# An attention and cosine-gated MLP kernel on one core: first k in fp32 by hardware queues, single-bank blocks of h, four output accumulators, a new order of loads

## The chip, the core and the metric

The kernel runs on one core of a Trainium2 chip. The time is device microseconds of one execution. The engines are TensorE (PE; its weight loads are the row PEld), VectorE (DVE), ScalarE (ACT), GpSimd (POOL) and SyncE (SP). Each works through its own list of instructions in order; semaphores order the engines among each other. DMAs are issued from SP and ACT (hardware queues, shown as hardware_dynamic) and from POOL (software queue). Casting fp32 to bf16 while loading is done on POOL's queue alone in this kernel.

## What is computed

Two attention steps, then a two-layer MLP without bias whose gate is a cosine:

```python
def sm_attn(qq, kk, vv):                        # scale = 1/sqrt(64)
    s = scale * np.matmul(qq, kk.transpose(0, 1, 3, 2))
    a = np.exp(s - s.max(-1, keepdims=True))
    return np.matmul(a / a.sum(-1, keepdims=True), vv)
p_packed = sm_attn(p, k, v)                     # p: 8 x 8 x 32 x 64; q, k, v: 8 x 8 x 576 x 64
x = sm_attn(q, p_packed, p_packed)              # then heads side by side: 4608 x 512
h = x @ w_in                                    # 512 x 2048
out = (h * np.cos(h)) @ w_out                   # 2048 x 512
```

Inputs and the output are fp32 in HBM; matmuls are bf16 into fp32 accumulators.

## The kernel before

There are 8 batches of 576 rows. A batch goes through these steps, each a function of the kernel:

- `load` brings k, q or v of a batch as bf16, 96 partitions x 8 heads x 384. `pe_T` (24 transposes on PE into PSUM, three groups of 8, each copied out by an engine that is named) or `xbar` (a transposing DMA issued on SP) makes kT and qT. `permute_v` reorders v.
- `s1`: scores of p against k, exponentials on ACT with their sums. `a1_pe`, `a1_one` or `a1_xbar` transposes them. `pp` multiplies by v and gives ppT (two copies on one engine, two on another). `ppw(b, n)` multiplies ppT by a quarter of w_in, so that PPW holds p_packed times w_in, 2048 columns.
- `s2`: scores of q against p_packed, exponentials. `sums2` and `normalise` divide by the sums, through Ln and Exp on ACT, and give a2n.
- `h_mm(b, fc)`: block fc of 16 of h, transposed: 128 features x 576 rows, as 4 matmuls of 288 columns (2 contraction halves y, 2 halves e of the rows) into a PSUM tile of two banks; ACT takes Sin with a phase of pi/2 (L254), VectorE multiplies it with h into gT (L257). After blocks 7 and 15 POOL copies the last 64 of the 576 rows to `joint`, in which two batches share a chunk of 128 rows.
- `out_gen(b)`: the output product, chunks of 128 rows, 16 matmuls of 512 columns each into one accumulator (L303), then a copy to SBUF and DMAs on SP. It is a generator: `fill(n)` takes n matmuls from it at a chosen place, `set_filler(b)` finishes the last batch's and starts a new one.

The order is written out by hand. First batches 0 and 1 up to their scores; then 16 blocks of h(0), with the rest of ppw(0) behind blocks 1, 5 and 8, pp(1) behind 10, the transposes of q1 behind 11 to 13, and 2 output matmuls behind 14 and 15; then s2(1) to normalise(1) with 22 output matmuls among them; then `slot(1, ...)`: 16 blocks of h(1), behind each its share of output matmuls of batch 0 and what its list of hooks names. The stages of batches 2 to 7 follow the same pattern, h(s) with the output of s − 1.

PSUM has 8 banks: pool A, three tiles of two banks each (`psa`), in turn; pool O, two tiles of one bank (`bank`, the accumulators, some transposes). A tile is taken again when all that read it before have finished.

POOL's list is at first: k0, v0, identity, q0, k1, p, w_in 0 to 2, v1, w_in 3, q1, w_out 0 to 3, p, k2, permute of v1, and later q2, k3, v2. xbar of k2, q2 and k3 stand on SP during h(1); a copy on POOL (`gate`, L444) waits for kT of batch 3, and behind it on POOL stand the load of q3, the permute of v2 and the loads of v3 and k4.

Of the kernel before, what the change touches and what calls it, by code (L numbers as in the profile page):

```python
# [8 lines left out]
FP32 = mybir.dt.float32  # L9
BF16 = mybir.dt.bfloat16  # L10
AF = mybir.ActivationFunctionType
# [4 lines left out]
def kernel(  # L16
# [10 lines left out]
    nc = tc.nc  # L27
# [19 lines left out]
    cos_pool = ctx.enter_context(tc.tile_pool(name="cos", bufs=3))  # L47
    o_pool = ctx.enter_context(tc.tile_pool(name="o", bufs=4))
    small = ctx.enter_context(tc.tile_pool(name="small", bufs=3))
    A = ctx.enter_context(tc.tile_pool(name="psA", bufs=3, space=PSUM))  # L50
    O = ctx.enter_context(tc.tile_pool(name="psO", bufs=2, space=PSUM))

    ctx.enter_context(tc.manual_schedule())
# [21 lines left out]
        else:  # L75
            eng.tensor_copy(out=out, in_=in_)  # L76

    def psa(dt=FP32):
        return A.tile([128, 2, 512 if dt == FP32 else 1024], dt, name="psA", tag="A")
# [161 lines left out]

    def h_mm(b, fc):
        if fc == 0:
            gT[b] = g_pool.tile([128, NFC, S], BF16, name="gT", tag="gT")
            if b % 2 == 0:
                joint[b // 2] = j_pool.tile([128, NFC, 128], BF16, name="joint", tag="joint")
        ps = psa()
        for y in range(2):
            for e in range(2):
                nc.tensor.matmul(ps[:, e, 0:HS], PPW[b][:, y, fc * 128:(fc + 1) * 128],  # L250
                                 a2n[b][:, y, e * HS:(e + 1) * HS], start=(y == 0), stop=(y == 1))
        cs = cos_pool.tile([128, S], BF16, name="cosT")
        csv = cs.rearrange("p (e x) -> p e x", e=2)
        ACT.activation(out=csv, in_=ps[:, :, 0:HS], func=AF.Sin, bias=PI_HALF)  # L254

        def rest():
            V.tensor_tensor(out=gT[b][:, fc, :].rearrange("p (e x) -> p e x", e=2),  # L257
                            in0=ps[:, :, 0:HS], in1=csv, op=ALU.mult)
# [4 lines left out]
        return rest  # L263

    n_out = [0]

# [13 lines left out]
    def n_chunks(b):  # L280
        return 5 if b % 2 and b < B - 1 else 4
# [11 lines left out]
                q.dma_start(out=rows[:, cols], in_=osb[a:z, cols])  # L293

    def out_gen(b):
        groups = [(0, 1), (2,), (3,)] if b == 0 else [(c,) for c in range(n_chunks(b))]
        for grp in groups:
            pss = {c: O.tile([128, DM], FP32, name="ot", tag="ot") for c in grp}
            for f0 in range(0, NFC, 4):
                for c in grp:  # L300
                    for fc in range(f0, f0 + 4):
                        w = joint[b // 2][:, fc, :] if c == 4 else gT[b][:, fc, c * 128:(c + 1) * 128]
                        nc.tensor.matmul(pss[c], w, w_out_bf[:, fc, :],  # L303
                                         start=(fc == 0), stop=(fc == NFC - 1))
                        if fc == NFC - 1:
                            osb = o_pool.tile([128, DM], FP32, name="osb")
                            copy((V, ACT)[n_out[0] % 2], osb, pss[c])
                            n_out[0] += 1
                            for a, z, rows in pieces_of(b, c):
                                nc.sync.dma_start(out=rows, in_=osb[a:z, :])  # L310
                        yield

    filler = [None, 0]
# [44 lines left out]
    for t in a1:  # L358
        V.memset(t[:, :, :, TP:128], 0.0)

    warm(7)
    dup_p(0, 2, V)
    pack_p(0, 1)
    warm(9)
    pe_T("k", 0, (V, ACT, V))
    s1(0)
    permute_v(0, V)
    load("v", 1)
    load_w_in(3)
    warm(3)  # L370
    a1_pe(0)
    warm(2)
# [1 line left out]
    pp(0)  # L374
    pe_T("q", 0, (V, ACT, V))
    load("q", 1)
    for n in range(4):
        load_w_out(n)
    G.dma_start(out=p_raw[:, 4:, :], in_=p_rows[:, 4:, :])
    s2(0)  # L380
    warm(3)
    dup_p(2, 4, V)
    sums2(0, 0)
    sums2(0, 1)
    pe_T("k", 1, (V, V, V))
# [6 lines left out]
    a1_one(1)  # L392
    rest_ppw()
    recips(1)
    load("k", 2)
    permute_v(1)
    for fc in range(NFC):
        h_mm(0, fc)()
        if fc in (1, 5, 8):
            ppw(0, 1 + fc // 4, (ACT, V), own=True)  # L400
        if fc == 10:
            pp(1, own=True, engs=(ACT, ACT))
        if fc in (11, 12, 13):
            pe_T("q", 1, (V, ACT, V), (fc - 11,), own=True)
        if fc == 13:
            set_filler(0)
        if fc >= 14:
            fill(2)

    def slot(s, hooks, keep=0, heavy={}):  # L410
        left = filler[1] - keep
        weight = [1 + heavy.get(fc, 0) for fc in range(NFC)]
        for fc in range(NFC):
            h_mm(s, fc)()
# [18 lines left out]
    ppw(1, 0, V)  # L433
    load("q", 2)
    load("k", 3)
    load("v", 2)
# [7 lines left out]
    G.tensor_copy(out=gate, in_=xT["k", 3][0:1, 0, 0:1])  # L444
    load("q", 3)
    ppw(1, 1, V)
    normalise(1)
    fill(14)
    slot(1, [(3, lambda: pw2(1, 2, (ACT, V))), (6, lambda: pack_p(2, 5)), (8, lambda: pack_p(5, B)),
             (8, lambda: (permute_v(2), load("v", 3), load("k", 4)))], 4)  # L450

    fill(1000)
    set_filler(1)
# [96 lines left out]
```

## Time and profile before

| | us |
|---|---|
| median of 3 runs | 254.21 (254.09 to 254.35) |
| span of the profiled execution | 252.3 |
| PE busy in it | 233.3 (92%), 1981 matmuls |
| ACT busy | 170.5 (68%) |
| DVE busy | 163.0 (65%) |
| POOL busy | 58.4 (23%) |
| DMA engines | 37.67 MB, mean 149 GB/s |
| first matmul of h(0), h(1), s1(2) | 22.73, 45.71, 63.89 |

The profile is one execution on the chip. Times in it count from the span's start. A line such as L254 is a line of the kernel before. A group names engine, operation, what it writes and reads, the shapes, how often, busy time, mean duration, and the idle time of the engine just before with what ended it. Matmul ends are modelled. The span is that of the execution's first to last instruction, and the runs' times lie somewhat above it.

### The profile page before, as it was taken

To read this page: it belongs to the slowest core of one execution; us is meant where nothing else is said; L and a number is where in the kernel's file an instruction comes from. 1 tells how busy PE (TensorE), PEld (TensorE's weight loads), DVE (VectorE), ACT (ScalarE), POOL (GpSimd) and SP (SyncE) were. 2 spreads that over 40 slices of the span, in tenths; PEclk is the share of its full clock that TensorE was granted. 3 is DMA by queue.
4 is the path that set the end of the run, shared out by engine and by line. 5 is a ranking of instruction groups with operands and counts; after the bars stand their busy time and mean duration, and the time that the engine had idled before them with its cause. 6 is when DMAs were issued, how large, how long until landed. Compare 5 with 4: busy or idle time off the path is not lost.

```text
span 252.3 us, 4989 instructions
## 1 busy us (share of the span) xinstructions
PE 233.3 (92%) x1981; PEld 130.7 (52%) x2014; DVE 163.0 (65%) x245; ACT 170.5 (68%) x285; POOL 58.4 (23%) x71
## 2 busy tenths in 40 slices
PE   8786888999969999999999998999899999999993
PEld 3453463566435554465446553565356554665452
DVE  2548996789376977477847675479556874876110
ACT  2366888857558788878886667887877585873000
POOL 8442604200362243104313105020500000000000
PEclk9999999999999999999999999999999999999998
DMA  6999999999999989999999994979471112112133
GB/s 91 202 211 205 205 207 226 200 186 149 191 208 198 176 175 212 220 204 164 225 173 181 180 182 99 175 141 196 97 144 44 42 44 70 36 34 62 50 83 83
DMA packets 65270, 37.67 MB, mean 149 GB/s; under 512 B 37872, under 2 KB 60656, under 8 KB 65248
## 3 DMA queue, kind: packets, MB, share of 16 engines
q0 software_dynamic: 23184, 18.81, 48.8%
q1 hardware_dynamic: 41904, 18.42, 36.8%
q8 instruction: 15, 0.25, 0.4%
q10 hardware_dynamic: 160, 0.13, 0.2%
q14 instruction: 7, 0.06, 0.1%
HBM read 37.22 MB, written 9.44 MB: 185 GB/s over the span
## 4 chain that ended last, share of the span: by engine, by line
PE 74%; DVE 8%; ACT 7%; DMA 5%; issue 2%; POOL 2%; DVEq 0%; POOLq 0%; ACTq 0%
PE ot L303 42%; PE psA L250 22%; DMA w_in_bf<-in_moe_w_in_dram 5%; DVE gT L257 5%; PE psA L201 3%; ACT cosT L254 3%; PE psA L177 2%; PE psA L227 1%; PE ot L289 1%; ACT a2u L219 1%; ACT L489 1%; DVE rs L147 1%; PE psA L128 1%; DVE osb L76 1%; DVE PPW L76 1%
## 5 line engine op out<-in xcount | busy, mean ns | idle before, releaser
L303 PE MATMUL ot<-w_out_bf,gT 128*128 128x512 bf16 x483 | 126.9, 380 | 2.1 <-issue 1.3
L257 DVE TENSOR_TENSOR gT<-psA,cosT 128x576 bf16<-128x576 f32 x128 | 94.1, 754 | 31.1 <-ACT cosT L254 30.0
L254 ACT ACTIVATE cosT<-psA 128x576 bf16<-128x576 f32 x128 | 82.7, 652 | 29.8 <-PE psA L250 28.1
L250 PE MATMUL psA<-a2n,PPW 128*128 128x288 bf16 x512 | 84.0, 286 | 2.5 <-DVE PPW L76 1.0
L303 PEld LDWEIGHTS <-gT 128*128 128x128 bf16 x512 | 48.0, 98 | 42.6 <-issue 6.1
L250 PEld LDWEIGHTS <-PPW 128*128 128x128 bf16 x512 | 49.1, 98 | 36.5 <-issue 3.8
L76 DVE CAST PPW<-psA 128x1024 bf16<-128x1024 f32 (+1 forms) x23 | 25.8, 1128 | 12.1 <-PE psA L201 12.1
L261 POOL COPY joint<-gT 128x512 bf16<-128x512 bf16 x16 | 9.8, 614 | 88.7 <-DVE gT L257 88.7
L76 DVE COPY osb<-ot 128x512 f32<-128x512 f32 (+1 forms) x19 | 12.8, 671 | 16.9 <-PE ot L303 13.8
L74 ACT COPY osb<-ot 128x512 f32<-128x512 f32 (+1 forms) x18 | 10.3, 571 | 18.7 <-PE ot L303 14.1
L76 POOL COPY vp<-vbf 96x3072 bf16<-96x3072 bf16 x7 | 19.2, 2750 | 1.6 <-DMA vbf<-in_v_dram 1.6
L237 DVE SCALAR_TENSOR_TENSOR a2n<-a2u,r,lns 128x576 bf16<-128x576 bf16 x16 | 12.4, 813 | 9.6 <-ACT lns L235 9.6
L229 ACT ACTIVATE lns<-psA 128x576 f32<-128x576 f32 x16 | 10.3, 651 | 5.7 <-PE psA L227 5.3
L137 ACT ACTIVATE a<-psA 128x576 bf16<-128x576 f32 x16 | 10.2, 648 | 5.0 <-PE psA L128 5.0
L303 PE MATMUL ot<-w_out_bf,joint 128*128 128x512 bf16 x46 | 12.4, 380 | 0.1
L201 PE MATMUL psA<-w_in_bf,ppT 64*32 64x512 bf16 x224 | 10.4, 381 | 1.5 <-DVE gT L257 1.1
L219 ACT ACTIVATE a2u<-psA,rs 128x576 bf16<-128x576 f32 x16 | 11.0, 736 | 1.2 <-PE psA L128 1.1
L254 ACT ACT_TABLE_LOAD x8 | 10.3, 1283 | 0.1
L74 ACT CAST ppT<-psA 64x128 bf16<-64x128 f32 x24 | 6.2, 259 | 6.1 <-PE psA L103 2.9
L235 ACT ACTIVATE lns<-lns 128x576 f32<-128x576 f32 x16 | 10.0, 678 | 0.0
L341 PE MATMUL ot<-wz 128*128 128x512 bf16 x24 | 8.1, 472 | 1.5 <-DVE wz L353 1.2
L74 ACT CAST PPW<-psA 128x1024 bf16<-128x1024 f32 (+1 forms) x9 | 7.2, 826 | 2.6 <-PE psA L201 2.6
(71 smaller groups left out, 143.4 us busy)
## 6 DMA issues: line engine op xcount, KB each, us to landing
kbf<-in_k_dram POOLq DMA_DIRECT2D x8, 576.0 KB, 12.2
vbf<-in_v_dram POOLq DMA_DIRECT2D x8, 576.0 KB, 7.4
qbf<-in_q_dram POOLq DMA_DIRECT2D x8, 576.0 KB, 9.6
out_dram<-osb SPq DMA_DIRECT2D x24, 192.0 KB, 2.6
out_dram<-osb SPq DMA_DIRECT2D x22, 128.0 KB, 2.4
w_in_bf<-in_moe_w_in_dram POOLq DMA_DIRECT2D x4, 512.0 KB, 16.5
w_out_bf<-in_moe_w_out_dram POOLq DMA_DIRECT2D x4, 512.0 KB, 20.9
out_dram<-osb SPq DMA_DIRECT2D x26, 64.0 KB, 2.1
```

Of the source, the lines that this page charges most:

```text
L74: ACT.copy(out=out, in_=in_)
L76: eng.tensor_copy(out=out, in_=in_)
L137: ACT.activation(out=a1[b % 2][:, y, :, 0:TP].rearrange("p (e m) x -> p e m x", e=2), in_=ps[y][:, :, 0:HS].rearrange("p e (m x) -> p e m ...
L201: nc.tensor.matmul(ps[y][32 * x:32 * x + 32, :], ppT[b % 2][r, 2 * x + y, :], w_in_bf[r, x, n * 512:(n + 1) * 512], start=True, stop=True)
L219: ACT.activation(out=a2u[b][:, y].rearrange("p (e x) -> p e x", e=2), in_=ps[y][:, :, 0:HS], func=AF.Exp, scale=rs1[b][:, y:y + 1])
L229: ACT.activation(out=lns[b][:, y].rearrange("p (e x) -> p e x", e=2), in_=ps[:, :, 0:HS], func=AF.Ln)
L235: ACT.activation(out=lns[b][:, y], in_=lns[b][:, y], func=AF.Exp, scale=-1.0)
L237: V.scalar_tensor_tensor(out=a2n[b][:, y], in0=a2u[b][:, y], scalar=r1[b][:, y:y + 1], in1=lns[b][:, y], op0=ALU.mult, op1=ALU.mult)
L250: nc.tensor.matmul(ps[:, e, 0:HS], PPW[b][:, y, fc * 128:(fc + 1) * 128], a2n[b][:, y, e * HS:(e + 1) * HS], start=(y == 0), stop=(y == 1))
L254: ACT.activation(out=csv, in_=ps[:, :, 0:HS], func=AF.Sin, bias=PI_HALF)
L257: V.tensor_tensor(out=gT[b][:, fc, :].rearrange("p (e x) -> p e x", e=2), in0=ps[:, :, 0:HS], in1=csv, op=ALU.mult)
L303: nc.tensor.matmul(pss[c], w, w_out_bf[:, fc, :], start=(fc == 0), stop=(fc == NFC - 1))
```

## The change

- k of batch 0 comes as fp32 in two halves of the heads, on SP's and ACT's hardware queues, into a tile (`kraw`) of the pool of gT. `k0_T` casts it with four copies (two on VectorE, two on ACT) and transposes it in four groups of 6, two groups to a psA tile.
- In batches 0 and 1 a block of h has 512 rows (`h_one`): 2 matmuls of 512 columns into one bank; a psA tile serves two blocks. The last 64 rows of all 16 blocks go in one step (`h_rest`): 32 matmuls of 64 columns into one psA tile, one Sin and one multiply of 1024 columns, straight into `joint`. h_rest(0) is behind block 1 of h(1), h_rest(1) behind block 15.
- The pool A is three tags of one tile each; `psa` goes round over the list `pairs`. `out_gen(0)` runs its four chunks together, four matmuls of each in turn: two accumulators in O, two in the halves of tile 2, which leaves `pairs` until the last chunk is copied out. 16 output matmuls stand in h(0), two behind each of blocks 6 to 13.
- pp(1) and the transposes of q1 move behind h(0). ppw(0, 2) and ppw(0, 3) stand behind blocks 5 and 9 and use psA.
- Transposes of k2 and q2 go to PE, as hooks of h(1); their xbar DMAs are gone.
- POOL's order: w_in 0 and 1, a quarter of w_out, w_in 2 and 3, then v1, q1, three quarters of w_out, p, k2; later q2, v2, k3. The permute of v2 and the load of v3 come before the gate for kT of batch 3.
- Warm-up matmuls (`warm`): 9 become 5, and 3 behind s2(0) go.

```diff
-    A = ctx.enter_context(tc.tile_pool(name="psA", bufs=3, space=PSUM))
+    A = ctx.enter_context(tc.tile_pool(name="psA", bufs=1, space=PSUM))
...
+    pairs, turn = [0, 1, 2], [0]
+    def psa(dt=FP32, at=None):
+        if at is None:
+            turn[0] += 1
+            at = pairs[turn[0] % len(pairs)]
+        return A.tile([128, 2, 512 if dt == FP32 else 1024], dt, name="psA", tag=f"A{at}")
...
+    def h_one(b, fc):
+        if fc == 0:
+            g_tile(b)
+        if fc % 2 == 0:
+            held_pair[0] = psa()
+        ps = held_pair[0][:, fc % 2, :]
+        for y in range(2):
+            nc.tensor.matmul(ps, PPW[b][:, y, fc * 128:(fc + 1) * 128], a2n[b][:, y, 0:512],
+                             start=(y == 0), stop=(y == 1))
+        cs = cos_pool.tile([128, 512], BF16, name="cosT")
+        ACT.activation(out=cs, in_=ps, func=AF.Sin, bias=PI_HALF)
+        V.tensor_tensor(out=gT[b][:, fc, 0:512], in0=ps, in1=cs, op=ALU.mult)
+
+    def h_rest(b):
+        t = psa()
+        for fc in range(NFC):
+            for y in range(2):
+                nc.tensor.matmul(t[:, fc // 8, (fc % 8) * 64:(fc % 8) * 64 + 64],
+                                 PPW[b][:, y, fc * 128:(fc + 1) * 128], a2n[b][:, y, 512:576],
+                                 start=(y == 0), stop=(y == 1))
+        cs = cos_pool.tile([128, 2, 512], BF16, name="cosR", bufs=1)
+        ACT.activation(out=cs, in_=t, func=AF.Sin, bias=PI_HALF)
...
-        groups = [(0, 1), (2,), (3,)] if b == 0 else [(c,) for c in range(n_chunks(b))]
+        groups = [(0, 1, 2, 3)] if b == 0 else [(c,) for c in range(n_chunks(b))]
         for grp in groups:
-            pss = {c: O.tile([128, DM], FP32, name="ot", tag="ot") for c in grp}
+            pss = {c: O.tile([128, DM], FP32, name="ot", tag="ot") for c in grp[:2]}
+            if len(grp) > 2:
+                pairs.remove(2)
+                held = psa(at=2)
+                pss |= {c: held[:, i, :] for i, c in enumerate(grp[2:])}
...
+                            if len(grp) > 2 and c == grp[-1]:
+                                pairs.append(2)
...
-    load("k", 0)
+    kraw = g_pool.tile([TP, H, C * D], FP32, name="kraw", tag="gT")
+    for q, h0 in ((nc.sync, 0), (ACT, 4)):
+        q.dma_start(out=kraw[:, h0:h0 + 4], in_=k[0, h0:h0 + 4].rearrange("h (p c) d -> p h (c d)", c=C))
...
-    for n in range(3):
-        load_w_in(n)
+    load_w_in(0)
+    load_w_in(1)
+    load_w_out(0)
+    load_w_in(2)
+    load_w_in(3)
...
+    def k0_T():
+        kb = bf["k", 0] = bf_pool.tile([TP, H, C * D], BF16, name="kbf", tag="kbf", bufs=2)
+        t = xT["k", 0] = att_pool.tile([128, H * 3, TP], BF16, name="kT", tag="kT", bufs=2)
+        flat, ps = kb.rearrange("p h x -> p (h x)"), {}
+        for g, eng in ((0, V), (2, ACT), (1, V), (3, ACT)):
+            copy(eng, kb[:, 2 * g:2 * g + 2], kraw[:, 2 * g:2 * g + 2])
+        tiles = [psa(BF16), psa(BF16)]
+        for i, (g, eng) in enumerate(((0, V), (2, ACT), (1, V), (3, V))):
+            ps = tiles[i // 2][:, i % 2, :]
...
     for fc in range(NFC):
-        h_mm(0, fc)()
-        if fc in (1, 5, 8):
-            ppw(0, 1 + fc // 4, (ACT, V), own=True)
-        if fc == 10:
-            pp(1, own=True, engs=(ACT, ACT))
-        if fc in (11, 12, 13):
-            pe_T("q", 1, (V, ACT, V), (fc - 11,), own=True)
-        if fc == 13:
+        h_step(0, fc)
+        if fc == 1:
+            ppw(0, 1, (ACT, V), own=True)
+        if fc in (5, 9):
+            ppw(0, 1 + fc // 4, (ACT, V))
+        if fc == 6:
             set_filler(0)
-        if fc >= 14:
+        if 6 <= fc < 14:
             fill(2)
...
+    pp(1)
     ACT.preload_act_table_set(EXP_SET)
+    pe_T("q", 1, (V, ACT, V))
+    load("q", 2)
     s2(1)
...
-    fill(8)
+    fill(5)
     sums2(1, 0)
     sums2(1, 1)
-    xbar("k", 2)
-    xbar("q", 2)
+    ppw(1, 0, V)
+    fill(6)
+    normalise(1)
+    ppw(1, 1, V)
+    fill(9)
     xbar("k", 3)
...
+    slot(1, [(1, lambda: h_rest(0)), (3, lambda: pw2(1, 2, (ACT, V))), (5, lambda: pack_p(2, 5)),
+             (6, tk("k", 2, 0)), (7, tk("k", 2, 1)), (8, tk("k", 2, 2)), (9, lambda: pack_p(5, B)),
+             (10, behind_k3),
+             (11, tk("q", 2, 0)), (12, tk("q", 2, 1)), (13, tk("q", 2, 2)), (15, lambda: h_rest(1))], 4)
```

Line numbers above 300 differ between the two kernels. In the changed one L284 are the matmuls of `h_one`, L287 its Sin, L288 its multiply, L295 the matmuls of `h_rest`, L430 the transposes of `k0_T`, L183 the matmuls of `pp` and L353 the output matmuls.

More of the change, by code (lines that the diff above doesn't have):

```diff
@@ L76, in copy @@
             eng.tensor_copy(out=out, in_=in_)
-    def psa(dt=FP32):
-        return A.tile([128, 2, 512 if dt == FP32 else 1024], dt, name="psA", tag="A")
+    pairs, turn = [0, 1, 2], [0]
[4 more added lines that the diff above has]
+        return A.tile([128, 2, 512 if dt == FP32 else 1024], dt, name="psA", tag=f"A{at}")
     def load(n, b):
@@ L243, in h_mm @@
         if fc == 0:
-            gT[b] = g_pool.tile([128, NFC, S], BF16, name="gT", tag="gT")
-            if b % 2 == 0:
-                joint[b // 2] = j_pool.tile([128, NFC, 128], BF16, name="joint", tag="joint")
+            g_tile(b)
         ps = psa()
@@ L263, in h_mm, with g_tile, h_step @@
         return rest
+    held_pair = [None]
+    def g_tile(b):
+        gT[b] = g_pool.tile([128, NFC, S], BF16, name="gT", tag="gT")
+        if b % 2 == 0:
+            joint[b // 2] = j_pool.tile([128, NFC, 128], BF16, name="joint", tag="joint")
+    def h_one(b, fc):
+        if fc == 0:
+            g_tile(b)
+        if fc % 2 == 0:
[16 more added lines that the diff above has]
+        ACT.activation(out=cs, in_=t, func=AF.Sin, bias=PI_HALF)
+        j0 = (b % 2) * 64
+        V.tensor_tensor(out=joint[b // 2][:, :, j0:j0 + 64],
+                        in0=t.rearrange("p a (f x) -> p (a f) x", x=64),
+                        in1=cs.rearrange("p a (f x) -> p (a f) x", x=64), op=ALU.mult)
+    def h_step(b, fc):
+        if b < 2:
+            h_one(b, fc)
+        else:
+            h_mm(b, fc)()
     n_out = [0]
@@ L359 @@
         V.memset(t[:, :, :, TP:128], 0.0)
+    def k0_T():
[7 more added lines that the diff above has]
+            ps = tiles[i // 2][:, i % 2, :]
+            for j in range(6):
+                o = 6 * g + j
+                nc.tensor.transpose(ps[:, j * TP:(j + 1) * TP], flat[:, o * 128:(o + 1) * 128],
+                                    ident[0:TP, 0:TP])
+            copy(eng, t[:, 6 * g:6 * g + 6].rearrange("p a x -> p (a x)"), ps[:, 0:6 * TP])
     warm(7)
@@ L363 @@
     pack_p(0, 1)
-    warm(9)
-    pe_T("k", 0, (V, ACT, V))
+    warm(5)
+    k0_T()
     s1(0)
@@ L368 @@
     load("v", 1)
-    load_w_in(3)
     warm(3)
@@ L376 @@
     load("q", 1)
-    for n in range(4):
+    for n in range(1, 4):
         load_w_out(n)
     G.dma_start(out=p_raw[:, 4:, :], in_=p_rows[:, 4:, :])
+    load("k", 2)
     s2(0)
-    warm(3)
-    dup_p(2, 4, V)
+    pe_T("k", 1, (V, V, V), own=True)
     sums2(0, 0)
     sums2(0, 1)
-    pe_T("k", 1, (V, V, V))
+    dup_p(2, 4, V)
     pack_p(1, 2, bank(BF16))
@@ L394 @@
     recips(1)
-    load("k", 2)
     permute_v(1)
     for fc in range(NFC):
-        h_mm(0, fc)()
-        if fc in (1, 5, 8):
-            ppw(0, 1 + fc // 4, (ACT, V), own=True)
-        if fc == 10:
-            pp(1, own=True, engs=(ACT, ACT))
-        if fc in (11, 12, 13):
-            pe_T("q", 1, (V, ACT, V), (fc - 11,), own=True)
-        if fc == 13:
+        h_step(0, fc)
[4 more added lines that the diff above has]
+        if fc == 6:
             set_filler(0)
-        if fc >= 14:
+        if 6 <= fc < 14:
             fill(2)
@@ L413, in slot @@
         for fc in range(NFC):
-            h_mm(s, fc)()
+            h_step(s, fc)
             quota = (left * sum(weight[:fc + 1])) // sum(weight) - (left + keep - filler[1])
@@ L429, in tk, with behind_k3 @@
         return lambda: pe_T(n, b, (V, V, V), (i,))
+    pp(1)
     ACT.preload_act_table_set(EXP_SET)
+    pe_T("q", 1, (V, ACT, V))
+    load("q", 2)
     s2(1)
-    ppw(1, 0, V)
-    load("q", 2)
+    load("v", 2)
     load("k", 3)
-    load("v", 2)
     dup_p(4, 2 * B, G)
-    fill(8)
+    fill(5)
     sums2(1, 0)
     sums2(1, 1)
-    xbar("k", 2)
-    xbar("q", 2)
-    xbar("k", 3)
[L444 to L450, printed above, removed]
+    ppw(1, 0, V)
[3 more added lines that the diff above has]
+    fill(9)
+    xbar("k", 3)
+    def behind_k3():
+        permute_v(2)
+        load("v", 3)
+        G.tensor_copy(out=gate, in_=xT["k", 3][0:1, 0, 0:1])
+        load("q", 3)
+        load("k", 4)
+    slot(1, [(1, lambda: h_rest(0)), (3, lambda: pw2(1, 2, (ACT, V))), (5, lambda: pack_p(2, 5)),
+             (6, tk("k", 2, 0)), (7, tk("k", 2, 1)), (8, tk("k", 2, 2)), (9, lambda: pack_p(5, B)),
+             (10, behind_k3),
+             (11, tk("q", 2, 0)), (12, tk("q", 2, 1)), (13, tk("q", 2, 2)), (15, lambda: h_rest(1))], 4)
     fill(1000)
```

## The prediction

> **What bounds the kernel now.** I first read the busy time by stretches, in the answer that cuts the span where the program's stages change (columns: stretch, length, then busy microseconds and instructions of PE, PEld, DVE, ACT, POOL, then granted clock, DMA share, GB/s).
>
> ```profile
> 16.30:22.68 6.38, 4.55 (x70) 2.92 (x69) 4.45 (x11) 5.49 (x11) 2.51 (x4) 1.00 1.24 205
> 22.68:38.50 15.82, 13.33 (x143) 8.07 (x142) 14.55 (x25) 12.84 (x25) 5.64 (x5) 1.00 1.27 205
> 38.50:45.50 7.00, 6.24 (x58) 2.83 (x58) 4.86 (x6) 6.27 (x9) 2.85 (x4) 1.00 1.25 220
> 45.50:62.40 16.90, 16.41 (x124) 10.36 (x125) 13.75 (x22) 11.44 (x19) 1.60 (x2) 1.00 1.33 173
> 62.40:79.50 17.10, 14.51 (x152) 6.84 (x153) 10.55 (x15) 11.13 (x21) 6.57 (x8) 1.00 1.10 204
> ```
>
> h(0) fills 22.68 to 38.50, and VectorE binds it (14.55 of 15.82). h(1), 45.50 to 62.40, is bound by PE (16.41 of 16.90): 16 blocks in 16.3 us, about one a microsecond, because the Sin and the multiply of one block run under the matmuls of the next. The edits all fall before 62.40, save the order in which transfers are queued.
>
> Second, the chain of waits around 38 us, where one block of h runs alone, for the latency of a block (start, length, engine and line).
>
> ```profile
> 37.49 0.67 PE psA L250 x4
> 38.18 0.66 ACT cosT L254
> 38.86 0.77 DVE gT L257
> 39.68 0.37 PE psA L201
> ```
>
> From the first matmul of a block to the first PE instruction that may follow its multiply: 39.68 − 37.49 = 2.19 us, for 576 columns.
>
> Third, the timeline at 21 us, where a1_one transposes into the two halves (two banks) of one psA tile.
>
> ```profile
> 21.06 0.64 ACT L137 ACTIVATE a<-psA 128x576 bf16<-128x576 f32 x1
> 21.79 0.55 DVE L76 COPY a1T<-psA 96x768 bf16<-96x768 bf16 x1 [0.16 <-PE psA L169]
> 22.40 0.49 PE L169 MATMUL psA<-ident,a 128*96 128x128 bf16 x6 [0.65 <-DVE a1T L76]
> ```
>
> The input of the second half was ready at 21.70 (21.06 + 0.64), yet PE started at 22.40, 0.06 us after VectorE had finished copying the *first* half out of the *other* bank. Accesses of two engines to one tile are put in order for the tile, not for the bank. This is the row that decides the forecast.
>
> Fourth, the costs and one late transfer, from the page and the list of waits.
>
> ```profile
> L257 DVE TENSOR_TENSOR gT<-psA,cosT 128x576 bf16<-128x576 f32 x128 | 94.1, 754 | 31.1 <-ACT cosT L254 30.0
> L76 DVE COPY osb<-ot 128x512 f32<-128x512 f32 (+1 forms) x19 | 12.8, 671 | 16.9 <-PE ot L303 13.8
> L74 ACT COPY osb<-ot 128x512 f32<-128x512 f32 (+1 forms) x18 | 10.3, 571 | 18.7 <-PE ot L303 14.1
> PEld L177 <- POOL vp L76: 2.5, 1, 2.5
> ```
>
> **The loop of a single-bank block.** h_one takes a two-bank psA tile for two blocks, and the changed kernel's instruction list has a wait on the first matmul of each odd block (L284) for the VectorE count of the even block's multiply (L288): the wait of L169 above, now once per pair. With 512 columns instead of 576, PE's part falls by 128/2.4 = 0.05 us (the 4x288 matmuls of a block stream in 0.48 us), the Sin from 0.65 to some 0.58 (the 571 ns row), the multiply from 0.754 to some 0.69 (671 ns row): 2.19 − 0.05 − 0.07 − 0.07 = 2.00 us from the start of an even block to that of the odd one. The PE time in between is 0.43 us of matmuls plus fillers; the rest is idle.
>
> **Start (k as fp32).** Removed: one POOL issue (0.89 us). Before, k landed at 7.41 and s1(0) ended at 9.68, 2.27 later. Now 1.18 MB go through two hardware queues; the store rows at the end reach 240 to 280 GB/s, so 4.5 us alone, from about 2.0: 6.5. v starts at 2.9 as k did and takes a share: up to 9.3. I take 8.0. Then four casts of 768 columns (VectorE 0.86 each at the rate of L336's 0.2 us for 128; ACT 0.80 as its kT copy) and four groups of transposes, of which the second of each tile waits for the copy of the first: s1(0) ends about 4.9 after landing (bounds 4.2 and 5.0), at 12.9 instead of 9.68. Taken back: three warm matmuls (0.6) after s2 that go, and the 0.2 us PE wait for w_in at 19.67, which lands earlier than needed now. h(0) starts +2.8 us later (bounds +0.8 and +4.5).
>
> **h(0).** Before, from its first matmul (22.73) to that of block 15 (37.49): 14.8 us. Now, in pairs: after an odd block the next even one can go at once (other tile), but its VectorE turn comes after the odd block's, so a pair takes 2.0 + 0.69 = 2.69; the PE work behind an odd block (two output matmuls 0.43) makes it 2.43 + 0.43 = 2.86. First block 2.65 (table load and PPW copies, as before), 7 pairs at 2.69 to 2.9, plus 0.7 of VectorE for each of three PPW copies, plus 0.8 where block 10 waits for block 9 because two tiles are left while the accumulators hold the third: 24.9. So +10.2. The 16 output matmuls (3.4 us) hide in the waits.
>
> **Between h(0) and h(1).** pp(1) (0.86) and the q(1) transposes (3 x 0.5) leave h(0) and stand alone: multiply of block 15, ppT copies 0.6 and 0.53 (ACT after VectorE, same tile), table 1.28, qT copy 0.80, s2 0.5, exponentials 1.37, then sums, Ln, Exp, a2n with 20 output matmuls under them. From block 15's start to h(1): 12.05 instead of 8.01 (37.49 to 45.50): +4.0.
>
> **h(1).** The instruction list has the accumulators holding the third tile until output 64 is done, which is after h(1). With two tiles and a hook in most steps, the even blocks wait for the odd block's multiply too, directly or behind a hook that does. So all 15 steps cost the loop: 15 x 2.03 = 30.5. At blocks 7, 9, 13 a transpose group waits first, then runs (0.5), then fillers (0.43): 3 x 0.93; the two PPW groups at 3 add 0.85; h_rest(0) (32 matmuls like L177's 24 in 0.86, so 1.15; its Sin and multiply of 1024 columns 1.1 and 1.2) adds 0.85. Sum 35.0 instead of 16.3: +18.6. The k2, q2 transposes themselves (48, some 3 us) are inside.
>
> **After block 15.** h_rest(1): 0.43 + 1.15 on PE, Sin 1.1, multiply 1.2; behind it on VectorE the copy of accumulator 2, and accumulator 3, in the same tile, can only finish after that copy; then ACT copies it and s1(2) waits. 6.6 us instead of 2.1 (61.79 to 63.89): +4.5.
>
> **Behind 64 us.** v2's permute is now issued long before pp(2): the 2.5 us wait falls away, −2.2 of it real (s2(2) at 73.54 could be at 71.4), −0.2 for the table load. Two transposing transfers less. Stages 2 to 7 are unchanged.
>
> **Sum against the profiled execution:** +2.8 +10.2 +4.0 +18.6 +4.5 −2.4 = +37.7 on its span of 252.3: 290.0. The median of the runs, 254.21, lies 1.9 above that span: **291.9 us**.
>
> The row L169 says that banks of one tile don't overlap here; "Perfetto Trace Analysis" of the Trainium skill, Matmuls, says that independent groups of matmuls should rotate through PSUM banks so that the evacuation of one overlaps the next. h_one does rotate banks, and by that rule the sum would be the first rival's; the row decides. For the clock the rows are given with the second rival; "TensorE: Matmul & The Clock Gate", Part 1, says that an idle window of about 3.4 us halves PE's clock, and that micro-idles between groups can make it swing. By that the sum would lie between forecast and second rival.
>
> **Rivals.** (1) *The halves of a pair overlap after all.* For: they are different banks, and nothing reads across. Against: L169, and the wait in the list. Then h(0) is VectorE's work, 2.2 us less than before (16 x 0.065, two qT copies): −2.2; the rest +2.8, +4.0, h(1) +2.2 (3 us of transposes, 2.3 of h_rest, less matmul columns and fillers), +3.0 after block 15, −2.4: +7.4, so 262. Chance 0.07. (2) *The clock halves in the gaps.* PE is idle for about 1.2 of each 2.0 us. For: the granted clock can fall, 0.96 over 233.40 to 252.30, where PE runs dry at the end; no stretch of before is so thin for so long. Against: in 16.30:22.68 PE was busy for 4.55 of 6.38 us and the clock stayed 1.00. Each loop gains 0.43, pairs of h(0) about 1.0: +17, so 309. Chance 0.08. (3) *Not slower:* PE alone sets the front, its idle time is filled by the output matmuls. In 22.68 to 62.40 PE is idle 39.7 − 36.0 = 3.7 us; new PE work is +3.0; so −0.7, and −2.4 behind: 251. It decides only if all waits of the front grow by less than 2.4 us; the first loop alone, h(0), exceeds that. Chance 0.02.
>
> **How the numbers follow.** Forecast 0.83, 283 to 301 by itself: a loop wrong by 0.1 us is 2 to 3 us over some 23 loops, the start −2.0 or +1.7, the hooks 3. The range 281 to 303 leaves rivals 1 and 3 and most of 2 outside. A measurement of this kernel can't tell less than 0.2% from no change; slower by more than that takes in the forecast and rivals 1 and 2: 0.97; faster 0.02, same 0.01.
>
> **What would show it.** In the changed profile: waits of PE at L284 on DVE L288, many, about 1.2 us each; PE busy about half in h(0) and h(1); block 0 to 15 of h(1) some 35 us; a gap of 2 to 3 us before the last output matmuls of batch 0; no wait of L183 on vp in batch 2; clock 1.00. If L284's waits sum to less than 10 us, the central step is wrong; if the granted clock falls to 0.5 there, rival 2.

## The result, and the profile after

| | before | after |
|---|---|---|
| median of 4 runs, us | 254.15 (254.07 to 254.35) | 301.19 (298.82 to 302.9) |
| span of the profiled execution, us | 252.3 | 298.6 |
| mean granted clock in it | 0.997 | 0.936 |
| PE busy, us | 233.3 (92%) | 251.3 (84%) |
| ratio of times | | 1.1844, 95% interval 1.1779 to 1.1909 |

The changed kernel is slower by 47 us; the forecast was 291.9, its range 281 to 303. Comparisons here leave disturbed runs out; one profile below (`before_vp_only`) is of such a run, and only its order of waits and its stages up to 76 us are read.

The page of the changed kernel, busy tenths of PE and granted clock in 40 slices of 7.5 us:

```profile
PE   5685576496665559999999999999999999999994
PEclk9579669989779888999999999999999999999999
```

PE is idle for some 40% of the time up to slice 15 (110 us) and full from there. In the same slices the clock falls, to 0.5 in one; before, it showed 9 in all but the last slice.

The waits of PE (engine, tile and line that waited, what ended it: us in all, times, longest):

```profile
PE psA L284 <- DVE gT L288: 20.4, 19, 2.0
PE psA L109 <- DVE gT L288: 3.5, 3, 1.4
PE psA L353 <- DVE osb L76: 2.5, 1, 2.5
PE psA L122 <- DVE p_bf L388: 2.2, 1, 2.2
```

The first line is the central step: the matmuls of `h_one` wait 20.4 us for its multiplies, where before no wait of that kind summed to over 1.1 us. The third is the copy of accumulator 2 that accumulator 3 waits for.

The timeline of PE in h(1), matmuls of `h_one` (start, length, then in brackets the idle time before and what ended it):

```profile
79.90 0.59 PE L284 MATMUL psA<-a2n,PPW 128*128 128x512 bf16 x2 [1.04 <-DVE gT L288]
...
81.90 0.59 PE L284 MATMUL psA<-a2n,PPW 128*128 128x512 bf16 x2 [0.65 <-DVE gT L288]
...
83.97 0.59 PE L284 MATMUL psA<-a2n,PPW 128*128 128x512 bf16 x2 [0.88 <-DVE gT L288]
...
87.13 1.06 PE L284 MATMUL psA<-a2n,PPW 128*128 128x512 bf16 x2
...
89.67 0.61 PE L284 MATMUL psA<-a2n,PPW 128*128 128x512 bf16 x2 [0.41 <-DVE gT L288]
```

The first three are blocks in a row: 2.00 and 2.07 us from one to the next, at full clock, and the even block at 81.90 waits like the odd ones. The pair of 87.13 takes 1.06 instead of 0.59: the clock is halved there, and the next block comes 2.54 later.

The busy time by stretches (columns as above, the last three granted clock, DMA share, GB/s); first the stages h(0), between, h(1), after block 15 and s1(2) with its stage, then parts of the start and of h(0):

```profile
27.70:54.90 27.20, 16.25 (x84) 5.49 (x82) 13.69 (x23) 10.79 (x20) 3.52 (x2) 0.81 0.88 146
54.90:67.45 12.55, 9.46 (x102) 4.66 (x99) 5.80 (x9) 8.15 (x12) 3.90 (x5) 0.86 0.72 105
67.45:105.30 37.85, 23.09 (x185) 10.86 (x184) 17.67 (x28) 12.05 (x20) 5.23 (x5) 0.86 0.42 54
105.30:110.44 5.14, 1.93 (x24) 0.88 (x20) 2.51 (x3) 1.82 (x4) 0.00 (x0) 0.98 1.27 222
110.44:125.00 14.56, 14.56 (x148) 6.74 (x148) 6.88 (x13) 9.91 (x19) 0.45 (x2) 0.89 0.64 138
...
10.00:16.00 6.00, 5.04 (x47) 3.19 (x47) 2.14 (x5) 2.01 (x5) 1.54 (x2) 0.50 1.31 209
...
30.00:35.00 5.00, 2.93 (x16) 0.97 (x16) 2.18 (x4) 1.99 (x4) 2.11 (x1) 0.67 1.31 205
35.00:40.00 5.00, 3.53 (x15) 0.81 (x14) 2.67 (x4) 2.46 (x5) 0.63 (x1) 0.50 1.25 206
```

No engine is full in h(0) and h(1): PE is busy for 16.25 of 27.20 and 23.09 of 37.85 us, some 60%, VectorE for half. That is a loop of waits, not an engine that binds.

The timeline of the start:

```profile
5.89 0.66 DVE L388 CAST p_bf<-p_raw 128x128 bf16<-128x128 f32 x2 [3.64 <-DMA p_raw<-in_p_dram]
6.16 1.56 ACT L74 CAST kbf<-kraw 96x768 bf16<-96x768 f32 x2 [3.65 <-DMA kraw<-in_k_dram]
...
6.61 0.28 PE L122 MATMUL psA<-ident,p_bf 128*128 128x128 bf16 x2 [2.24 <-DVE p_bf L388]
...
8.41 1.03 DVE L76 CAST kbf<-kraw 96x768 bf16<-96x768 f32 x2 [1.19 <-DMA kraw<-in_k_dram]
...
9.02 0.66 PE L430 MATMUL psA<-ident,kbf 96*128 96x96 bf16 x6 [1.03 <-DVE kbf L76]
```

p, 64 KB on SP's queue ahead of half of k, landed at 5.89. k's halves landed at 6.16 and 8.41, against 7.41 before.

Where the time went can be read from ACT's table loads: each stage begins with one (Sin for h, Exp for the scores). Their times give the length of each stage in every kernel:

| kernel | Sin of h(0) at | h(0) | to h(1) | h(1), to s1(2) | to h(2) | rest | span | clock |
|---|---|---|---|---|---|---|---|---|
| before | 21.81 | 17.04 | 5.70 | 20.05 | 13.84 | 173.86 | 252.3 | 0.997 |
| after | 26.77 | 30.55 | 7.79 | 45.30 | 13.50 | 174.69 | 298.6 | 0.936 |
| own_tile | 26.59 | 20.46 | 7.94 | 38.63 | 12.82 | 174.66 | 281.1 | 0.957 |
| two_acc | 26.68 | 29.90 | 9.89 | 34.86 | 11.56 | 174.71 | 287.6 | 0.947 |
| own_tile_two_acc | 25.15 | 20.20 | 9.65 | 23.34 | 11.55 | 174.61 | 264.5 | 0.987 |
| before_h512 | 22.05 | 28.51 | 5.64 | 30.24 | 11.55 | 173.91 | 271.9 | 0.969 |
| k_cast | 24.18 | 31.42 | 7.94 | 47.07 | 12.94 | 174.75 | 298.3 | 0.925 |
| more_warm | 25.14 | 30.69 | 6.40 | 48.94 | 13.40 | 174.63 | 299.2 | 0.930 |
| two_acc_pp_back | 26.59 | 19.78 | 7.03 | 23.35 | 11.55 | 174.70 | 263.0 | 0.998 |
| two_acc_k_cast | 21.84 | 25.68 | 9.77 | 23.35 | 11.56 | 174.80 | 267.0 | 0.971 |
| two_acc_576 | 27.33 | 19.41 | 9.70 | 22.04 | 11.56 | 174.66 | 264.7 | 0.966 |
| two_acc_all_back | 22.20 | 26.70 | 7.03 | 22.04 | 11.56 | 174.77 | 264.3 | 0.978 |

Of the 46.3 us between the two spans, 38.8 lie in h(0) and h(1), 5.0 at the start, 2.1 between, and the rest of the kernel is as it was.

### The profile page after: what moved, and what is told of

Same layout as the page of the kernel before. It is cut to its first block, busy times and chain, and to the rows that moved or that the text cites. A ratio compares the mean times of both kernels' runs of the same rounds, so it can differ in the third digit from the quotient of the medians.

```text
span 298.6 us, 5114 instructions
## 1 busy us (share of the span) xinstructions
PE 251.3 (84%) x2055; PEld 132.1 (44%) x2055; DVE 167.9 (56%) x258; ACT 173.0 (58%) x287; POOL 55.2 (18%) x66
## 4 chain that ended last, share of the span: by engine, by line
PE 73%; DVE 11%; ACT 10%; DMA 2%; issue 2%; SPq 0%; ACTq 0%; DVEq 0%
PE ot L353 36%; PE psA L254 15%; PE psA L284 7%; DVE gT L288 6%; ACT cosT L287 4%; DMA kraw<-in_k_dram 2%; PE psA L207 2%; PE psA L134 2%; PE psA L353 2%; PE psA L183 2%; PE psA L233 1%; PE ot L335 1%; DVE PPW L76 1%; ACT a2u L225 1%; ACT L567 1%
## 5 line engine op out<-in xcount | busy, mean ns | idle before, releaser
L353 PE MATMUL ot<-w_out_bf,gT 128*128 128x512 bf16 x480 | 128.5, 387 | 0.0
L261 DVE TENSOR_TENSOR gT<-psA,cosT 128x576 bf16<-128x576 f32 x96 | 70.9, 755 | 27.1 <-ACT cosT L258 26.3
L258 ACT ACTIVATE cosT<-psA 128x576 bf16<-128x576 f32 x96 | 62.2, 652 | 21.7 <-PE psA L254 19.3
L353 PEld LDWEIGHTS <-gT 128*128 128x128 bf16 x512 | 48.4, 100 | 49.6 <-issue 14.1
L254 PE MATMUL psA<-a2n,PPW 128*128 128x288 bf16 x384 | 62.9, 286 | 0.9 <-DVE PPW L76 0.6
L254 PEld LDWEIGHTS <-PPW 128*128 128x128 bf16 x384 | 37.5, 98 | 26.9 <-issue 2.3
L287 ACT ACTIVATE cosT<-psA 128x512 bf16<-128x512 f32 x32 | 19.1, 598 | 40.4 <-PE psA L284 40.3
L284 PE MATMUL psA<-a2n,PPW 128*128 128x512 bf16 x64 | 22.7, 445 | 20.4 <-DVE gT L288 20.4
L288 DVE TENSOR_TENSOR gT<-psA,cosT 128x512 bf16<-128x512 f32 x32 | 22.1, 691 | 31.0 <-ACT cosT L287 31.0
L76 DVE CAST PPW<-psA 128x1024 bf16<-128x1024 f32 (+1 forms) x25 | 27.2, 1093 | 16.2 <-PE psA L207 15.5
L265 POOL COPY joint<-gT 128x512 bf16<-128x512 bf16 x12 | 7.4, 613 | 91.9 <-DVE gT L261 91.9
L284 PEld LDWEIGHTS <-PPW 128*128 128x128 bf16 x64 | 6.6, 107 | 33.4 <-issue 29.3
L89 POOL DMA_DIRECT2D qbf<-in_q_dram x8 | 6.2, 775 | 47.3 <-PE psA L109 28.3
L235 ACT ACTIVATE lns<-psA 128x576 f32<-128x576 f32 x16 | 10.2, 651 | 7.3 <-PE psA L233 6.8
L207 PE MATMUL psA<-w_in_bf,ppT 64*32 64x512 bf16 x240 | 11.7, 394 | 1.8 <-DVE gT L288 1.1
L353 PE MATMUL ot<-w_out_bf,joint 128*128 128x512 bf16 x48 | 12.8, 379 | 0.0
L353 PE MATMUL psA<-w_out_bf,gT 128*128 128x512 bf16 x32 | 10.5, 417 | 2.5 <-DVE osb L76 2.5
## 6 DMA issues: line engine op xcount, KB each, us to landing
w_out_bf<-in_moe_w_out_dram POOLq DMA_DIRECT2D x4, 512.0 KB, 18.6
```

Of the source, the lines that this page charges most:

```text
L207: nc.tensor.matmul(ps[y][32 * x:32 * x + 32, :], ppT[b % 2][r, 2 * x + y, :], w_in_bf[r, x, n * 512:(n + 1) * 512], start=True, stop=True)
L235: ACT.activation(out=lns[b][:, y].rearrange("p (e x) -> p e x", e=2), in_=ps[:, :, 0:HS], func=AF.Ln)
L284: nc.tensor.matmul(ps, PPW[b][:, y, fc * 128:(fc + 1) * 128], a2n[b][:, y, 0:512], start=(y == 0), stop=(y == 1))
L287: ACT.activation(out=cs, in_=ps, func=AF.Sin, bias=PI_HALF)
L288: V.tensor_tensor(out=gT[b][:, fc, 0:512], in0=ps, in1=cs, op=ALU.mult)
L353: nc.tensor.matmul(pss[c], w, w_out_bf[:, fc, :], start=(fc == 0), stop=(fc == NFC - 1))
```

## The experiments

Times are medians; ratios are to the kernel before, on the same chip in the same job.

**A tile for each block.** The bank stays single, but each block takes its own psA tile; the second bank of it lies idle.

```diff
-        if fc % 2 == 0:
-            held_pair[0] = psa()
-        ps = held_pair[0][:, fc % 2, :]
+        ps = psa()[:, 0, :]
```

> The changed kernel with one edit: a block of h in batches 0 and 1 takes a psA tile for itself and uses half of it, so no two blocks share a tile. Theory (accesses of two engines to one tile are ordered for the whole tile, and the odd block's matmuls so wait for the even block's multiply): h(0) from its first block to block 15 falls from 26.5 us to 14 to 17; in h(1) hooks still take every second tile of two, so about 9 of 15 steps keep the loop of 2.0 us and h(1) falls from 36.8 to 25 to 28; 276 to 284 us. Rival 1 (the work that was moved or added binds, pp(1), transposes of q1, k2, q2, h_rest): less than 5 us gained, 296 or more. Rival 2 (the halved clock is what costs): PE stays as idle as now and the time stays over 290.

281.85 us, ratio 1.1056 (1.099 to 1.1121): 19 us back. h(0) falls by 10.1 us, and h(1) with the stretch ahead of it by 6.5 (the table). The waits of PE, the line of `h_one`:

```profile
PE psA L282 <- DVE gT L286: 5.8, 12, 1.0
```

20.4 us of this wait became 5.8, with the same matmuls, Sin and multiplies: with a tile of its own the odd block no longer waits for the even one's multiply. By first matmuls h(0) took 16.2 us from block 0 to 15 and h(1) 28.3, where 14 to 17 and 25 to 28 were expected. The edit also leaves every second bank unused; a kernel in which the two banks of a pair are two tiles wasn't run. That the order is kept for the tile is read from the record, in which PE is released by the multiply of the other bank. What is left comes from two tiles while the accumulators hold the third (both edits together, below, leave 0.4).

**Two accumulators, as before.**

```diff
-        groups = [(0, 1, 2, 3)] if b == 0 else [(c,) for c in range(n_chunks(b))]
+        groups = [(0, 1), (2,), (3,)] if b == 0 else [(c,) for c in range(n_chunks(b))]
```

> The changed kernel with one edit: the output of batch 0 in the groups (0, 1), (2,), (3,) of before, so that psA keeps its three tiles and no accumulators share a tile. Theory: the odd blocks keep their wait, the even ones of h(1) lose theirs; h(1) falls from 36.8 to 27 to 30 us, the wait of 2.5 us before the last output matmuls of batch 0 goes; 288 to 293 us. Rival (the halves of a pair don't matter, the tile that the accumulators hold does): the L284 waits go altogether, 275 or less.

289.64 us, ratio 1.1375 (1.1328 to 1.1422). h(0) hardly falls (0.65), h(1) with the stretch ahead of it by 8.3. (The two are taken together, since in kernels with two accumulators ACT copies the first of them out just ahead of the Sin's table load, which moves that mark by 1.8 to 2.0 us and makes the output matmuls wait for 0.67.) The waits:

```profile
PE psA L284 <- DVE gT L288: 22.2, 20, 2.0
```

They sum to as much as in the changed kernel, so the pairs still stall with three tiles. Of the even blocks of h(1), which were to lose their wait, 4, 8, 10 and 14 still wait, 0.3 to 0.6 us each, and h(1) took 30.5 us from block 0 to 15, just above the 27 to 30 expected. The gain is elsewhere: the hooks' transposes and the copy of accumulator 2 (3.5 and 2.5 us in the list of the changed kernel) no longer wait there, and less of the front runs at the low clock (0.947 against 0.936 over the span).

**Both edits.**

> The changed kernel with both edits: a psA tile for each block in batches 0 and 1, and the output of batch 0 in the groups of before, so three tiles throughout. Theory: no block waits for the one before it; h(1) falls to 18 to 22 us; 264 to 271 us, the rest over 254 being the start (5), the stage of pp(1) between h(0) and h(1) (4) and the added PE work of h(1) with h_rest(1) at its end (4 to 8). Rival (the two edits heal the same waits, 281.9 and 289.6 don't add): 276 or more.

266.72 us, ratio 1.0463 (1.0417 to 1.0509): 34.5 of the 47 us are undone by these two edits, 10.4 in h(0) and 20.1 in h(1) with the stretch ahead of it. There they give more together than alone (6.5 and 8.3): a block stops waiting only when neither its partner nor the accumulators are in its way. What is left over the kernel before is 12.5 us (11.5 against its runs in this job). Two lines from the waits of PE, the blocks and a new one:

```profile
PE psA L282 <- DVE gT L286: 0.4, 2, 0.2
PE ot L351 <- DMA w_out_bf<-in_moe_w_out_dram: 2.1, 1, 2.1
```

Of 20.4 us of waits for the multiply 0.4 are left. The second line is a wait in h(0) for a quarter of w_out; it bears on the last four runs.

**The single-bank blocks alone, put into the kernel before** (`h_one` and `h_rest` for batches 0 and 1, with their hooks; nothing else).

```diff
-        h_mm(0, fc)()
+        h_step(0, fc)
...
+(1, lambda: h_rest(0)), ... (15, lambda: h_rest(1))
```

> The kernel before with one part of the change: h_one with two blocks in a tile, and h_rest, in batches 0 and 1; everything else stays. Theory: h(0) +9 to +12, h(1) +7 to +10, +2 to +4 behind block 15; 272 to 282 us. Rival (blocks in single banks cost only their added weight loads on PE, some 1 us a batch): 255 to 258.

274.38 us, ratio 1.0771 (1.0726 to 1.0817). The waits in it:

```profile
PE psA L280 <- DVE gT L284: 18.9, 17, 2.2
```

The same wait at nearly the same sum: one part of the change makes 20 us by itself, 11.5 in h(0) and 10.2 in h(1). The column to h(2) fell by 2.3 though nothing was edited there: with h(1) longer, vp is there when pp(2) wants it.

**The permute of v2 and the load of v3 ahead of the gate, in the kernel before.**

```diff
+    def behind_k3():
+        permute_v(2)
+        load("v", 3)
+        G.tensor_copy(out=gate, in_=xT["k", 3][0:1, 0, 0:1])
+        load("q", 3)
+        load("k", 4)
...
-             (8, lambda: (permute_v(2), load("v", 3), load("k", 4)))], 4)
+             (8, behind_k3)], 4)
```

> The kernel before with one part of the change: the permute of v2 and the load of v3 stand on POOL ahead of the gate for kT of batch 3. Theory: the wait of pp(2) for vp (2.5 us) goes and nothing takes its place: 251.5 to 252.5 us. Rival (another wait ends last there, or the earlier load of v3 collides with the transposing DMAs): 253.5 to 254.5.

255.38 us, ratio 1.0022 (0.9995 to 1.0049): nothing gained, the rival's answer. pp(2) no longer waits for vp, but a line further on in the timeline of PE shows what is late next:

```profile
71.63 0.44 PE L128 MATMUL psA<-kT,P 64*32 64x288 bf16 x16 [1.71 <-DMA kT<-kbf]
```

The load of v3 and the transposing DMA of k3 were issued at 62.27 and 61.87 and shared the DMA engines; s1(3) waits 1.71 us for kT. In the kernel before, the same DMA was issued at 61.74 without that load, and the copy on POOL that waits for it ran at 66.78; here it ran at 71.64.

**The permute alone ahead of the gate, the loads behind it.** The edit is the one above without its `load("v", 3)`, which stands between the loads of q3 and k4.

> The kernel before with only the permute of v2 ahead of the gate for kT of batch 3; the loads of q3, v3 and k4 stay behind the gate. Theory (in the run with the load of v3 ahead too, that load shared the DMA engines with the transposing transfer of k3 and s1(3) waited 1.7 us for it): kT of batch 3 lands at about 66.8 again, pp(2) doesn't wait, 251.5 to 252.5 us. Rival (s1(3) or the next stage waits for something else): 253.5 to 254.5.

255.21 us, ratio 1.0013 (0.9971 to 1.0055): again no change that can be told, and less certain than the others. The Sin of h(2) came at 76.22 instead of 78.44, the predicted 2.2 us. But the waits of PE then hold a new one:

```profile
PE psA L177 <- DMA a1T<-a: 3.0, 1, 3.0
```

pp(3) waits 3.0 us for the transposing DMA of a1T. That the gain went there is what this one profile suggests, no more.

**The first k as before** (`load("k", 0)`, nine warm matmuls and `pe_T` in place of `kraw`, five and `k0_T`).

```diff
-    kraw = g_pool.tile([TP, H, C * D], FP32, name="kraw", tag="gT")
...
+    load("k", 0)
...
-    warm(5)
-    k0_T()
+    warm(9)
+    pe_T("k", 0, (V, ACT, V))
```

> The changed kernel with the first k as before: cast while loading, on POOL's queue, ahead of v, 9 warm-up matmuls and three groups of transposes. Theory (the fp32 way is late by itself: p and k share the hardware queues, PE runs dry, casts and the second half's waits follow): the first matmul of h(0) at 22.7 to 23.5 instead of 27.7, the granted clock 1.00 up to there, 295 to 297 us. Rival (w_in's landing sets the start of h(0) whatever k does): 299 or more.

299.97 us, ratio 1.1746 (1.1684 to 1.1808): a miss. h(0) came 2.6 us earlier, not 4.2 or more. What is missing is near a new wait of 1.9 us, for k1:

```profile
PE ot L109 <- DMA kbf<-in_k_dram: 1.9, 1, 1.9
```

And the 2.6 us were gone at s1(2) (110.61 against 110.41): h(0) took 0.9 us more, at a clock of 0.78 instead of 0.83, and h(1) 1.8 more, at 0.82 instead of 0.88.

**More warm matmuls at the start** (7 to 12 and 5 to 9).

```diff
-    warm(7)
+    warm(12)
...
-    warm(5)
+    warm(9)
```

> The changed kernel with 12 and 9 warm-up matmuls instead of 7 and 5, so that PE has work where it ran dry before 9 us. Theory (part of the late start is the halved clock, 0.60 from 10 to 20 us): the clock stays near 1.00 there and h(0) starts 1.0 to 2.0 us earlier, 299 to 300.5 us. Rival (the start is bound by the landing of p and k and by VectorE's and ACT's copies, and the clock costs nothing): h(0) starts at 27.7 as before or later.

301.18 us, ratio 1.1807 (1.1756 to 1.1858). h(0) began 1.6 us earlier, as expected, with the clock at 0.72 instead of 0.50 over 10 to 16 us. The end did not move, so the total is a miss (299 to 300.5 was expected). From h(0) on the code is that of the changed kernel; the stretch ahead of h(1) took 1.4 us less, at a clock of 1.00 instead of 0.78, and h(1) 3.6 more, at 0.75 instead of 0.88. The time won early was lost again where the clock fell further.

The last four were made from the kernel with both edits (266.72) and looked for the 12.5 us that were left. That kernel has the wait of 2.1 us for w_out in h(0), so its h(0) hides a start that comes up to 2.1 us later, and a stage that loses the wait looks shorter than the edit made it.

**pp(1) and the transposes of q1 back in h(0).**

```diff
+        if fc == 10:
+            pp(1)
+        if fc in (11, 12, 13):
+            pe_T("q", 1, (V, ACT, V), (fc - 11,))
...
-    pp(1)
...
-    pe_T("q", 1, (V, ACT, V))
```

> The kernel with a psA tile for each block and two accumulators (266.72 us), with pp(1) and the transposes of q1 put back behind blocks 10 to 13 of h(0), here in psA tiles. Theory: standing alone between h(0) and h(1) they cost about 4 us (pp 0.86, three transpose groups of 0.5, and their copies and table load behind each other); within h(0), which VectorE binds, PE's part is free and only the copies that go to VectorE count: 262 to 264.5. Rival: h(0) grows by as much as the stage behind it shrinks: 266 to 268.

264.78 us, ratio 1.0396 (1.036 to 1.0432): 1.9 us gained, just outside the theory's range and outside the rival's. By the table the two stages together fall by 3.0 (9.65 to 7.03, and h(0) 20.20 to 19.78). But h(0) began 1.4 later in this profile, and its wait for w_out is 0.57 instead of 2.12: without this wait the two stages fall by 1.5, since h(0) grew by 1.1 of the 2.6 by which the stage behind it shrank.

**The first k as before**, with the same edit as above.

> The same kernel (266.72 us) with the first k loaded by the casting queue as in the kernel before. Alone in the changed kernel this edit brought h(0) 2.6 us earlier and only 1.2 us at the end, with the granted clock at 0.50 in places. Theory: that loss was the clock's; here the clock is 0.987, so the 2.6 us stay: 263 to 265. Rival: what the start gains is lost at a wait behind it whatever the clock: 266 to 267.5.

268.7 us, ratio 1.053 (1.0483 to 1.0577): slower, which neither side expected. h(0) began 3.3 us earlier and took 5.5 longer. One wait is 2.6 longer than in the kernel that it was made from (2.12):

```profile
PE ot L351 <- DMA w_out_bf<-in_moe_w_out_dram: 4.7, 1, 4.7
```

The rest lies behind it: from the end of the wait to the Sin of h(1) it takes 19.0 us instead of 16.4, and the first pairs of matmuls there take 1.0 to 1.1 us instead of 0.59.

**Blocks of 576 rows everywhere**, no `h_rest`.

```diff
-        if b < 2:
-            h_one(b, fc)
-        else:
-            h_mm(b, fc)()
+        h_mm(b, fc)()
...
-(1, lambda: h_rest(0)), ... (15, lambda: h_rest(1))
```

> The same kernel (266.72 us) with blocks of 576 rows (h_mm) in batches 0 and 1 too, and without the two steps for the last 64 rows. Theory: the single-bank blocks with tiles of their own cost only the two h_rest steps, some 2 us within h(1) and 2 to 4 us behind its block 15, less about 1 us of VectorE in h(0): 261 to 264. Rival: the blocks cost more than that (more and shorter instructions on ACT and VectorE): below 260; or nothing: 266 to 268.

266.0 us, ratio 1.0433 (1.0386 to 1.048): in total no gain, the rival's answer by a little. By stage h(0) is 0.8 and h(1) 1.3 us shorter, and the start of this profile 2.2 longer, with p landing at 6.69 and the clock at 0.50 again. There is no wait for w_out in it (2.12 before), so without this wait h(0) is 1.3 longer, not shorter, and the late start cost little.

**All three.**

> The same kernel (266.72 us) with all three of these edits. What is left of the change is the order of loads, the transposes of k2 and q2 on PE (48, some 3 us, without two transposing DMAs) and the early output matmuls in h(0). Theory: 254.2 + 3 - 1 = 254 to 258, that is the parts add up. Rival: one wait stands behind all three, and two of the edits gain nothing together: 259 to 262. Below 253.5 it would beat the kernel before.

265.85 us, ratio 1.0432 (1.0395 to 1.0469): both ranges missed; the parts don't add up. The timeline of PE in h(0):

```profile
33.77 0.61 PE L348 MATMUL ot<-w_out_bf,gT 128*128 128x512 bf16 x2
34.21 0.65 PE L254 MATMUL psA<-a2n,PPW 128*128 128x288 bf16 x4
38.87 1.01 PE L348 MATMUL ot<-w_out_bf,gT 128*128 128x512 bf16 x2 [4.00 <-DMA w_out_bf<-in_moe_w_out_dram]
39.67 1.49 PE L183 MATMUL psA<-a1T,vp 96*128 96x64 bf16 x24
40.97 1.15 PE L254 MATMUL psA<-a2n,PPW 128*128 128x288 bf16 x4
```

With four accumulators the 16 output matmuls of h(0) use only the first quarter of w_out. With two, the ninth needs the second quarter, and PE waits 4.00 us for it; then the clock is halved (1.01, 1.49, 1.15 us where 0.59, 0.86 and 0.65 are usual). In the four kernels that show this wait it ends at 38.62, 38.57, 38.30 and 38.87, whenever h(0) began. The DMA engines moved 205 to 209 GB/s over 10 to 20, 20 to 30 and 30 to 38 us in these four, so the quarter's landing is nearly a fixed time, and a faster start only waits longer. Two accumulators with no more than 8 output matmuls in h(0) would avoid it; that wasn't run, and no kernel here beats the one before.

## Why the prediction was right, and where its sizes were off

Measured from first matmul to first matmul, as the prediction did (it took 45.50 for the start of h(1) before; the first matmul is at 45.71, which shifts 0.2 us from one step to the next):

| step | predicted | measured |
|---|---|---|
| start, to h(0) | +2.8 | +5.0 (27.74 − 22.73) |
| h(0), block 0 to 15 | +10.2 | +11.7 (26.50 − 14.76) |
| between | +4.0 | +5.0 (13.26 − 8.22) |
| h(1), block 0 to 15 | +18.6 | +20.7 (36.75 − 16.08) |
| block 15 to s1(2) | +4.5 | +4.1 (6.19 − 2.10) |
| behind s1(2) | −2.4 | −0.2 (188.2 − 188.4) |
| sum | +37.7 | +46.3 |

**The mechanism held.** The wait of L169, six transposes long in the kernel before, was the row that decided: `own_tile` took the sharing of a tile away and with it 10.1 of the 13.5 us by which h(0) had grown in the table, and `before_h512` made the stall alone. The loop at full clock was forecast at 2.00 us and is 2.00 to 2.07. That even blocks of h(1) wait too is in the timeline (81.90); with both edits nearly all of these waits go, with three tiles alone only some, since a hook that takes a tile makes an even block wait too. pp(1) and q1 standing alone were priced at 4.0; putting them back shortened the two stages by 3.0, of which 1.5 is a shorter wait for w_out, so about 1.5 of the 4.0 is shown.

"Perfetto Trace Analysis" of the Trainium skill, Matmuls, asks to rotate independent groups of matmuls through PSUM banks so that the evacuation of one overlaps the next. The runs say when that holds here: with two blocks in the banks of one tile the waits were 20.4 us in all, with a tile for each block 5.8, and 0.4 once a third tile was free.

**The term that was mis-sized is the clock.** The prediction took 1.00 and gave the clock's fall as a rival of its own, priced +17 over all loops, with 0.08. It fell in part: 0.81 in h(0), 0.86 between and in h(1), 0.89 behind. The sum was short by 8.6 us: 2.2 at the start, 1.5, 1.0 and 2.1 in the three stages, 2.2 behind, less 0.4. Other runs help to say how much of it is the clock.

- Behind: from the table load of s1(2) to that of h(2), `own_tile` and `two_acc` execute the same 124 matmuls: in 12.82 us at a clock of 0.90, in 11.56 at 1.00. So the predicted −2.4 is a true −2.3 there (13.84 to 11.56), of which the low clock takes 1.3 back; the rest of the kernel took another 0.8 (173.86 to 174.69), which no run here explains.
- Between and in h(1): `more_warm` has the same code there. The stretch ahead of h(1) took 6.40 us at 1.00 and 7.79 at 0.78, 1.4 apart, which covers the 1.0 of that stage. h(1) took 48.94 at 0.75 and 45.30 at 0.88, and 9 of its 16 blocks have their matmuls at 0.9 to 1.1 us instead of 0.59 in `more_warm`, 4 in the changed kernel; a straight line through the two, an estimate, gives 3.4 us for the 0.12 below 1.00, more than the 2.1 by which the stage was short.
- h(0): no run had this loop at 1.00, so its 1.5 is argued, not shown.
- Start: the same code gave the Sin of h(0) at 25.15 with the clock at 1.00 over 10 to 16 us (`own_tile_two_acc`), and at 26.77 with 0.50; 0.2 of this was there at the first transpose of k (8.83 and 9.02). The row of the clock alone isn't safe here: `two_acc_pp_back`, with the same start, shows 1.00 and has its Sin at 26.59. Twelve transposes of k took 1.12 us in it, as in the changed kernel, and 0.67 in `own_tile_two_acc`, so PE was slow there too; and its k came 0.8 later.

The four runs of the changed kernel point the same way: 298.82 us at a clock of 0.947, 302.9 at 0.925, and the other two between. By the prediction's own sign, a clock of 0.50, its second rival came in part. That the total stayed within the range is partly luck, since no term of the sum or of the range's working stood for the clock.

The prediction weighed 4.55 of 6.38 us busy at clock 1.00 against that rival, and that row was too weak: it held for 6 us, the two loops last for 26.5 and 36.8. "TensorE: Matmul & The Clock Gate" of the Trainium skill, Part 1, gives an idle window of about 3.4 us for the fall and says besides that micro-idles between groups can make the clock swing. The second sentence is what the trace shows: no wait of L284 is longer than 2.0 us, and the clock stood at 0.50 over 35 to 40 us.

**The start** was sized wrongly by two more things. p shares the queue and the DMA engines with k and landed at 5.89 instead of 2.67; the prediction had k late, not p, and PE's idle time for p (2.24 us) and k (1.03 us) is what stands ahead of the halved clock. k itself was taken at 8.0, and its later half came at 8.41. The casts cost less than taken (two of VectorE in 1.03 us, not 0.86 each).

**−2.4 behind 64 us** would not have come in the kernel before: there the two runs with the earlier permute gave 1.0022 and 1.0013. What the wait for vp hid was another DMA, kT for s1(3) or a1T for pp(3).

The other two rivals fell: the halves don't overlap (20.4 us of waits), and output matmuls did not fill PE's idle time (16.25 of 27.20 busy).

## What to carry to other kernels

A buffer split into parts was one buffer here to whatever orders the accesses; before packing two uses into one tile, look in the trace for any place where one engine writes one half while another reads the other, and see who waits. And where a planned stall leaves an engine idle for a large part of its time, here 40%, price its work at the lower clock too, not as a rival of all or nothing. When edits are undone one by one, look for the load that lands at a fixed time: behind it, gains don't add.

## What the runs showed of the hardware

- The granted clock fell to 0.50 with PE busy for 3.53 of 5.00 us, in waits of at most 2.0 us, and it was still 0.89 over 110.44 to 125.00 us, where PE ran without a gap (14.56 of 14.56 us).
- A load of 64 KB that lands 1.9 us after its issue when alone on the hardware queues took 5.1 us with 1.18 MB beside it there.
- A transposing DMA issued within 0.4 us of a load of 576 KB came 1.71 us too late for s1(3): what waits for it ran 9.8 us after its issue, and 5.0 after it without that load.
- The profile's granted clock can miss a slow stretch: `two_acc_pp_back` shows 1.00 over 10 to 16 us, while twelve transposes took 1.12 us there and 0.67 in a profile that was fast.
